# Input pieces, output-weight spreading and two-tile first matmuls in the opening of a planned attention-and-SoLU kernel

## The chip, the cores and the metric

The kernel runs on one core of a Trainium2 chip. The metric is device time in microseconds (us) of one launch; the median of 3 runs before the change is 1184.7 us. The engines are called PE (matmul; PEld is its weight load), DVE (vector), ACT (scalar), POOL (GpSimd) and SP (which issues the DMAs).

## The reference

There are four batches of 12608 tokens with 128 channels, 32 inducing points, and one feed-forward layer of width 1024 with a softmax gate (SoLU) and a layer norm.

```python
def mab(q, kv):                          # scale = 1 / sqrt(128)
    s = scale * (q @ kv.transpose(0, 2, 1))
    a = exp(s - s.max(-1)); a /= a.sum(-1) + 1e-09
    return a @ kv
x = mab(x, mab(I, x)).reshape(50432, 128)   # I: 32 inducing points per batch
h = x @ w_in                             # 128 -> 1024
e = exp(h - h.max(-1)); solu = h * e / (e.sum(-1) + 1e-09)
ln = (solu - mean(solu)) / sqrt(var(solu) + 1e-06) * g_ln
out = ln @ w_out                         # 1024 -> 128
```

w_in, w_out and g_ln come in the layout of the inputs; the two weight matrices are doubles of 1 MB each that the kernel rounds to float32 itself.

## The kernel before

**Work.** A batch is 99 tiles of 128 tokens. Part one (p1) loads a chunk of up to 16 tiles of x (12 in batch 0), turns them on PE, copies the turned tiles to SBUF (xT), makes the scores against the inducing points (L733), takes the maximum (L760, L766, L771, L792, L799), the exponent (ACT, L824), turns it back (L844), and gathers the weighted x (PE L850; DVE L882 adds it to acc). The turned x goes out to DRAM (xd) and comes back later as xT. When all chunks of a batch are through, combine (L910 to L936) divides by the sum (ACT accn, L915), makes h4 (DVE L919) and multiplies it by w_in (PE L933, copied to hs by ACT). Part two (p2) makes the second softmax of a chunk (PE L991, DVE L1001 and L1003, POOL L1006, ACT L1013) and turns the result into aT.

**The body.** For each tile: PE makes 1024 columns from aT and hs (L1233, "first matmuls"; K is 32 rows, so a tile takes two of the four row groups of the array), DVE multiplies and takes the minimum (hn, L1275), ACT takes the exponent (eu, L1286), POOL multiplies (L1290), ACT squares for the variance (L1301), DVE turns 32 x 32 blocks into vt (L1317). When a group of four tiles is turned, the products with w_out (L1473) follow in 32 steps for each of two pairs of row groups. A beat is one step on both pairs: eight matmul records, since each float32 matmul is recorded twice. Where only one pair has something to multiply, the step is a half beat. First matmuls, which use one pair, are issued with products on the other pair (`beats`, `whole`).

**Order.** No engine chooses at run time. The kernel yields operations with a cost, a priority (a low number goes first) and their predecessors to a Planner, which plays the four engines and SP through and writes the instructions down in that order; each engine then works through its list in order. What an instruction really waits for on the chip is only the data and buffers that it touches: the planner's tokens (BULK), events (loaded, turned) and priorities move instructions in the lists and make no wait of their own.

**The opening.** Until batch 0 is through part one, PSUM is eight small banks (bank_e). Batch 0's x is loaded with one DMA for 8 to 12 tiles. w_out is loaded, rounded on DVE, ACT and POOL (rounded), scaled by g_ln (ACT L492), its mean over the 1024 rows is taken on PE (L501) and subtracted on DVE (L506), and the 32-row quarters are spread over all partitions by PE (L544) and copied into wc by DVE and ACT (L522). All of that stands before handover, which closes the small banks and opens four two-bank tiles H for the body. Products need wc. Where the planner sees PE free for long it writes filler transposes (L557).

## Time and profile before

| | |
|---|---|
| median of 3 runs | 1184.7 us (1184.48 to 1186.08) |
| the profiled execution | 1182.92 us, of which the span of its instructions is 1181.1 us |
| PE, ACT, DVE, POOL busy | 97%, 93%, 91%, 90% of the span |
| first matmuls of the first tile | 52.87 us |
| first product with w_out | 76.74 us |
| mean granted PE clock | 0.994 |

A row of a timeline gives the start, the length, the engine, the line of the kernel, the operation and what it writes and reads; the brackets at its end say how long the engine idled before it and what ended that. Busy shares of all engines are high, so the question for each stretch is which wait ends last there.

### The profile page before, as it was taken

The numbers are of one execution on the slowest core, as the hardware profiler recorded it, in microseconds if no ns is written. First come the engines' busy times: TensorE is split into PE (matmuls) and PEld (weight loads), VectorE is DVE, ScalarE is ACT, GpSimd is POOL, SyncE is SP. The second block draws the span as 40 slices with busy tenths as digits, with TensorE's granted clock in tenths as the row PEclk, the third lists the DMA queues.
The fourth block names the chain that finished last, engine by engine and source line by source line (L and its number), as shares of the span: only waits on it lengthen the run. The fifth ranks groups of instructions, "written<-read, shape, count | busy, mean of one in ns | idle before, by whom it ended". The sixth has DMA issues, their size and how long they took to land.

```text
span 1181.1 us, 68196 instructions
## 1 busy us (share of the span) xinstructions
PE 1151.1 (97%) x30636; PEld 1055.0 (89%) x30636; DVE 1074.8 (91%) x1639; ACT 1102.6 (93%) x2191; POOL 1065.6 (90%) x612
## 2 busy tenths in 40 slices
PE   9999999999999999999999999999999999999996
PEld 7669989998889898999899999999988999999996
DVE  6799989898999899999899998999999999999981
ACT  5699899999999999999999999999999999999994
POOL 3399799898999989899899998989999999999994
PEclk9989999999999999999999999999999999999999
DMA  9532342522143433331423433341313131220103
GB/s 340 230 124 76 111 121 71 155 73 49 41 119 86 141 111 107 96 104 33 120 66 94 121 107 120 102 127 45 101 40 84 40 79 34 67 64 5 49 5 87
DMA packets 166884, 110.62 MB, mean 94 GB/s; under 512 B 78112, under 2 KB 131776, under 8 KB 166464
## 3 DMA queue, kind: packets, MB, share of 16 engines
q1 hardware_dynamic: 166592, 106.27, 31.0%
q8 instruction: 239, 3.92, 1.4%
q14 instruction: 53, 0.43, 0.1%
HBM read 53.51 MB, written 52.17 MB: 89 GB/s over the span
## 4 chain that ended last, share of the span: by engine, by line
PE 45%; POOL 23%; ACT 20%; issue 7%; DVE 3%; DMA 2%; SPq 0%; ACTq 0%; POOLq 0%; DVEq 0%
PE h L1473 32%; POOL eu L1290 16%; ACT sq L1301 9%; ACT eu L1286 6%; PE h L1233 4%; POOL spare L1290 3%; POOL spare L1547 3%; ACT spare L1286 1%; ACT xT L666 1%; ACT spare L1501 1%; PE h L850 1%; PE h L655 1%; ACT a L1013 1%; PE bank_e L557 1%; DMA dl<-dd 1%
## 5 line engine op out<-in xcount | busy, mean ns | idle before, releaser
L1473 PEld LDWEIGHTS h<-wc,vt 32*128 32x128 f32 (+1 forms) x25344 | 954.3, 185 | 45.8 <-issue 13.3
L1473 PE MATMUL h<-wc,vt 32*128 32x129 f32 (+1 forms) x25344 | 983.5, 273 | 10.4 <-ACT spare L1501 3.1
L1290 POOL TENSOR_TENSOR eu<-hn,eu 128x1024 f32<-128x1024 f32 x198 | 466.8, 2377 | 28.7 <-ACT eu L1286 27.7
L1233 PE MATMUL h<-hs,aT 32*128 32x512 f32 x1584 | 419.6, 607 | 6.0 <-DVE spare L1275 2.6
L1317 DVE STREAM_TRANSPOSE vt<-eu 128x1024 f32<-128x1024 f32 x327 | 397.7, 1229 | 11.4 <-POOL eu L1290 10.7
L1301 ACT ACTIVATE sq<-eu 128x1024 bf16<-128x1024 f32 x330 | 346.4, 1050 | 11.3 <-POOL eu L1290 6.5
L1290 POOL TENSOR_TENSOR eu<-spare,eu 128x1024 f32<-128x1024 f32 x132 | 311.7, 2379 | 11.2 <-ACT eu L1286 11.1
L1275 DVE TENSOR_SCALAR_CACHE_REDUCE hn<-h,rn 128x1024 f32<-128x1024 f32 x198 | 248.7, 1260 | 20.6 <-PE h L1233 12.2
L1275 DVE TENSOR_SCALAR_CACHE_REDUCE spare<-h,rn 128x1024 f32<-128x1024 f32 x198 | 248.2, 1260 | 20.7 <-PE h L1233 10.0
L1286 ACT ACTIVATE eu<-hn,nm 128x1024 f32<-128x1024 f32 x198 | 225.4, 1139 | 2.9 <-DVE hn L1275 2.7
L1290 POOL TENSOR_TENSOR spare<-spare 128x1024 f32<-128x1024 f32 x66 | 156.9, 2377 | 12.2 <-ACT spare L1286 12.2
L1286 ACT ACTIVATE eu<-spare,nm 128x1024 f32<-128x1024 f32 x132 | 150.4, 1140 | 2.3 <-DVE vt L1317 1.3
L1233 PEld LDWEIGHTS h<-hs,aT 32*128 32x128 f32 x1584 | 124.6, 186 | 27.5 <-DVE spare L1275 8.1
L1317 DVE STREAM_TRANSPOSE vt<-spare 128x1024 f32<-128x1024 f32 x65 | 80.0, 1231 | 2.0 <-POOL spare L1290 1.8
L1547 POOL TENSOR_TENSOR spare<-spare,fin 128x512 f32<-128x512 f32 x79 | 79.8, 1041 | 1.6
L1301 ACT ACTIVATE sq<-spare 128x1024 bf16<-128x1024 f32 x66 | 69.3, 1050 | 6.9 <-POOL spare L1290 5.3
L1286 ACT ACTIVATE spare<-spare,nm 128x1024 f32<-128x1024 f32 x66 | 75.2, 1140 | 0.4 <-DVE spare L1275 0.4
L1301 ACT ACTIVATION_READ_ACCUMULATOR sq<-eu 128x1 f32 x330 | 62.6, 190 | 0.0
L655 PE MATMUL h<-ident,xn 32*128 32x32 f32 x1188 | 53.6, 227 | 0.1
L655 PEld LDWEIGHTS h<-ident,xn 32*128 32x128 f32 x1188 | 51.1, 141 | 1.1 <-issue 0.8
L1501 ACT COPY spare<-h 128x774 f32<-128x774 f32 (+3 forms) x66 | 42.5, 646 | 9.3 <-PE h L1473 7.0
L666 ACT COPY xT<-h 128x1024 f32<-128x1024 f32 (+2 forms) x42 | 37.8, 900 | 1.1 <-PE h L655 1.1
(189 smaller groups left out, 849.6 us busy)
## 6 DMA issues: line engine op xcount, KB each, us to landing
out_dram<-spare SPq DMA_DIRECT2D x95, 256.0 KB, 3.3
xT<-xd SPq DMA_DIRECT2D x93, 256.0 KB, 3.8
xn<-in_x_dram SPq DMA_DIRECT2D x73, 256.0 KB, 3.7
xd<-xT SPq DMA_DIRECT2D x72, 256.0 KB, 2.6
dl<-dd SPq DMA_DIRECT2D x392, 1.0 KB, 2.3
xd<-vt SPq DMA_DIRECT2D x7, 768.0 KB, 10.2
spare<-in_x_dram SPq DMA_DIRECT2D x5, 768.0 KB, 9.3
dd<-qe SPq DMA_DIRECT2D x95, 4.0 KB, 2.1
```

What stands on the lines that cost most here:

```text
L557: nc.tensor.transpose(out=bank[:, :P], in_=ident, identity=ident)
L655: nc.tensor.transpose(out=tr[:, k * 512 + s * M : k * 512 + (s + 1) * M], in_=xn[r, s, :], identity=ident[r, r])
L666: lambda: nc.scalar.copy(xT.rearrange("c s (q t) -> c q s t", q=4)[:, 2 * w : 2 * w + 2, :n, :], tr.rearrange("c (k x) -> c k x", k=2)[:, ...
L1233: nc.tensor.matmul(hp[:, cols], lhsT=aT[rows, i // 2, :], rhs=hs[rows, cols], start=True, stop=True)
L1275: lambda: nc.vector.tensor_scalar(out=hn, in0=hp, scalar1=rn, scalar2=None, op0=ALU.mult, op1=ALU.min, accum_out=nm),
L1286: "ACT", 1133, lambda: nc.scalar.activation(e, hn, AF.Exp, bias=nm, scale=-1.0, accum_out=G["qe"][:, s, 1:2]), d, rel, srel,
L1290: d = yield Op("POOL", 2330, lambda: nc.gpsimd.tensor_tensor(out=e, in0=hn, in1=e, op=ALU.mult), de, prio=t + PR_MU)
L1301: "ACT", 1040, lambda: nc.scalar.activation(sq, e, AF.Square, scale=1.0 / 32.0, accum_out=G["qe"][:, s, 0:1]), d,
L1317: lambda: nc.vector.transpose(out=G["vtb"][:, : n * FF].rearrange("p (j s t) -> p j s t", j=M, s=n)[:, :, s, :], in_=e.rearrange("p (a f) ...
L1473: nc.tensor.matmul(op[:rows, a - 2 * w, :], lhsT=vt[q, k, :], rhs=wc[q, k, :], start=(k == 0), stop=(k == JB - 1))
L1501: return lambda: eng(to, at)
L1547: return lambda: eng.tensor_tensor(out=raw, in0=raw, in1=y[:, i0 : i0 + 4].unsqueeze(2).to_broadcast([rows, 4, C]), op=ALU.mult)
```

## The change

Seven things are changed together.

1. Batch 0's x is loaded in pieces of 4 tiles (256 KB), chunk after chunk, and a turn of 4 tiles needs only its own piece. The load of w_in stands after chunk 1 and that of w_out after chunk 4 (before: after chunk 3).
2. The mean of w_out, its subtraction and the spreading into wc move behind handover: they use tiles H of the body, two quarters to a tile, at priority WC_PR.
3. Until the first products are released (`flow["quiet"]`), the first matmuls of two tiles go out as one step on all four row groups (`mm1_two`, L1267 of the new kernel), and the turns of p1 and p2 are made on the whole array instead of by 32-row groups.
4. Products of a group are queued in the order of the groups (`began`), after wc is laid out.
5. The driver looks at the first unfinished group of each pair only.
6. In the planner: PE may pick an operation that is up to 100 ns late (SLACK), half beats weigh half in its picture of PE's clock (HALF), and four tiles instead of three are looked at for the next first matmuls (WINDOW_TILES).
7. Priorities: squares fall behind (PR_SQ from -4 to 6), fillers are written from 200 ns of idle time on, and w_out's steps and the weights' loads are moved. JS is an empty list, so the term with `wide` is always 0.

```diff
-FILL = 400
+FILL = 200
-LATE = -15
+LATE = -22
-PR_SQ = -4
+PR_SQ = 6
-SLACK = {"PE": 0, "ACT": 400, "DVE": 100, "POOL": 100, "SP": 0}
+SLACK = {"PE": 100, "ACT": 400, "DVE": 100, "POOL": 100, "SP": 0}
-WINDOW_TILES = 3
+WINDOW_TILES = 4
...
     def weights_out():
...
+        yield loaded[WOUT_AT]
         g = yield from rounded(wg2, w_out.bitcast(U32).rearrange("(k p) d -> p k d", p=P), conv2, None, conv2_free, WOUT_X)
...
-        yield turned[NP[0] - 1]
-        mp, rel = yield EARLY_PB.at(LATE)
+        if MEAN_H:
+            yield handed
+            where = H
...
+                hb, rel = yield H.at(WC_PR)
+                op = Op("PE", 950, None, d, rel, prio=WC_PR)
...
-        halves = [(0, GS), (GS, n)] if early and not k and n > GS else [(0, n)]
-        if not early:
-            halves = [(c, min(c + PIECE, n)) for c in range(0, n, PIECE)]
+        halves = [(c, min(c + PIECE, n)) for c in range(0, n, PIECE)]
+        if early and k:
+            yield loaded[k - 1]
...
-        if not early:
+        rows_only = not early and not flow["quiet"]
+        if rows_only:
             ways = [0, 1]
             for _ in range(2):
                 spawn(by_rows(ways), PRIO_P1(b, k))
-        for c0 in range(0, n if early else 0, most):
+        for c0 in range(0, 0 if rows_only else n, most):
...
-            mine = [p for q in stream for p in q if p["j"] < JB]
+            mine = [p for q in stream for p in [next((p for p in q if p["j"] < JB), None)] if p]
...
+                    if flow["quiet"] and len(left) > 1:
+                        two = [(s, part_of[b, ff_groups[j][0] + s]) for s in left[:2]]
...
+                        def mm1_two():
+                            hs = hT[b][1]
+
+                            for k in range(2):
+                                for (s, (ka, i)), hb in zip(two, (hp, hp2)):
+                                    r = i % 2 * 2
+                                    rows = slice((r + k) * M, (r + k + 1) * M)
+                                    cols = slice(k * 512, (k + 1) * 512)
+                                    aT = aT_of[(b, ka)]["aT"][0]
+                                    nc.tensor.matmul(hb[:, cols], lhsT=aT[rows, i // 2, :], rhs=hs[rows, cols], start=True, stop=True)
...
+        if turn_of[b, j]:
+            yield began[w][turn_of[b, j] - 1]
         yield PAIR[w].at(t)
+        yield wc_ready
+        flow["quiet"] = False
...
-        for e in (early_turned, wc_ready):
+        for e in (early_turned,) if MEAN_H else (early_turned, centred):
             d = yield e
             done += d
```

**PE, from w_in's product to the first matmuls of the body.** In the kernel before, the scores of the second p2 chunk (L991) are followed by the first matmuls of the tiles one by one (L1233, two rows of 512 columns for each tile, into one H tile each):

```order
L933 MATMUL bank_e_77<-w_in_sb,h_0_117 128x512
L557 MATMUL bank_e_72<-ident 128x128 x3
L1026 MATMUL bank_e_78<-ident,a_93 128x128 x2
L991 MATMUL h_730<-vt,h_0_117 32x256 x4
L1233 MATMUL h_732<-hs,aT_94 128x512 x2
L1233 MATMUL h_733<-hs,aT_94 128x512 x2
L1233 MATMUL h_730<-hs,aT_94 128x512 x2
L991 MATMUL h_731<-xT_86,h_0_117 32x512 x4
```

In the changed kernel the same place reads as follows (L959 is w_in's product, L1017 the scores, L1052 the turn of p2, L520 w_out's mean, L1267 the two-tile step):

```order
L959 MATMUL bank_e_78<-w_in_sb,h_0_117 128x512
L581 MATMUL bank_e_72<-ident 128x128 x3
L1052 MATMUL bank_e_79<-ident,a_93 128x128 x2
L1017 MATMUL h_709<-vt,h_0_117 32x256 x4
L520 MATMUL h_710<-hn_82,ones_mean 128x128 x8
L1267 MATMUL h_712<-hs,aT_94 128x512
L1267 MATMUL h_709<-hs,aT_94 128x512
L1052 MATMUL h_710<-ident,a_93 128x128 x4
```

The eight matmuls of the mean have moved from the opening to the place directly before the first matmuls, and two tiles share a step.

**DVE, from the second p2 chunk to the first group's transposes.** Before, hn of the first tiles (L1275) follows the maximum of the second p2 chunk at once:

```order
L1001 STREAM_TRANSPOSE s_1_90<-h_730 128x256
L1003 TENSOR_REDUCE mx_91<-s_1_90 128x8
L1275 TENSOR_SCALAR hn_81,nm_112<-h_732,rn_95 128x1024
L1275 TENSOR_SCALAR hn_80,nm_113<-h_733,rn_95 128x1024
L1095 TENSOR_REDUCE nr_92<-a_93 128x8
L1275 TENSOR_SCALAR hn_82,nm_114<-h_730,rn_95 128x1024
```

In the changed kernel (L1340 is hn, L525 the subtraction of w_out's mean, L1382 the transpose into vt, L543 a copy into wc):

```order
L1029 TENSOR_REDUCE mx_91<-s_1_90 128x8
L525 TENSOR_TENSOR hn_82<-h_710,hn_82 128x1024
L1124 TENSOR_REDUCE nr_92<-a_93 128x8
L1340 TENSOR_SCALAR hn_81,nm_112<-h_712,rn_95 128x1024
L1128 RECIPROCAL rn_97<-nr_92 128x8
L1340 TENSOR_SCALAR hn_80,nm_113<-h_709,rn_95 128x1024
L1027 STREAM_TRANSPOSE s_0_87<-h_711 128x512
L1029 TENSOR_REDUCE mx_88<-s_0_87 128x16
L1340 TENSOR_SCALAR spare,nm_114<-h_712,rn_95 128x1024
L1340 TENSOR_SCALAR spare,nm_115<-h_710,rn_95 128x1024
L1382 STREAM_TRANSPOSE vt<-eu 128x32x32
L543 COPY wc<-h_712 128x4x128
```

The subtraction now stands in front of the first hn, and copies into wc stand between the hn of the first tiles; the fourth transpose into vt comes after the tenth hn in both kernels.

**ACT, a stretch of the body after the first products.** Before (L1286 is the exponent, L1301 the square, L1072 a copy of turned aT):

```order
L1286 ACTIVATE eu,qe_106<-hn_80,nm_113 128x1024
L1072 COPY aT_96<-h_730 128x2x8x32
L1286 ACTIVATE eu,qe_106<-hn_82,nm_114 128x1024
L1301 ACTIVATE sq,qe_104<-spare 128x1024
L1286 ACTIVATE eu,qe_106<-spare,nm_115 128x1024
L1301 ACTIVATE sq,qe_106<-eu 128x1024 x3
```

In the changed kernel (L1351 is the exponent, L1366 the square, L691 a copy of turned x):

```order
L1351 ACTIVATE eu,qe_102<-spare,nm_112 128x1024
L1571 COPY spare<-h_711 128x2x3x129
L1351 ACTIVATE eu,qe_102<-hn_82,nm_114 128x1024
L1351 ACTIVATE spare,qe_102<-hn_81,nm_115 128x1024
L691 COPY xT<-h_709 128x2x16x32
L1366 ACTIVATE sq,qe_100<-eu 128x1024
L1366 ACTIVATE sq,qe_102<-eu 128x1024 x3
L1366 ACTIVATE sq,qe_102<-spare 128x1024
```

Squares have moved behind more exponents; over the whole list a square stands on average 3.1 exponents after its own instead of 2.6.

## Rows read from the trace of the kernel before

**Rows 1.** The page's first part: busy time of each engine, share of the span and instructions; and from its fourth part the shares of the engines in the chain that ended last.

```profile
PE 1151.1 (97%) x30636; PEld 1055.0 (89%) x30636; DVE 1074.8 (91%) x1639; ACT 1102.6 (93%) x2191; POOL 1065.6 (90%) x612
...
PE 45%; POOL 23%; ACT 20%; issue 7%; DVE 3%; DMA 2%; SPq 0%; ACTq 0%; POOLq 0%; DVEq 0%
```

**Rows 2.** Busy time of each engine by stretch: the stretch and its length, then PE, PEld, DVE, ACT, POOL with their instructions, the granted PE clock, the DMA share and GB/s.

```profile
20.00:30.00 10.00, 8.92 (x116) 6.49 (x114) 8.89 (x20) 7.05 (x17) 9.07 (x5) 1.00 1.05 400
30.00:40.00 10.00, 9.52 (x162) 7.73 (x163) 9.38 (x40) 6.08 (x19) 4.99 (x4) 1.00 1.01 419
40.00:50.00 10.00, 10.00 (x108) 7.42 (x107) 6.42 (x20) 5.51 (x18) 0.43 (x2) 1.00 0.46 176
...
60.00:70.00 10.00, 8.92 (x82) 3.81 (x79) 10.00 (x18) 9.78 (x20) 10.00 (x6) 0.93 0.37 127
```

**Rows 3.** DVE in order of time at the end of the opening.

```profile
41.02 0.22 DVE L792 TENSOR_SCALAR_CACHE_REDUCE small<-bank_e,m 128x4 f32<-128x4 f32 x1 [0.90 <-PE bank_e L771]
...
41.86 0.45 DVE L844 STREAM_TRANSPOSE spare<-spare 128x256 f32<-128x256 f32 x1 [0.42 <-ACT spare L824]
42.91 1.23 DVE L506 TENSOR_TENSOR hn<-bank_e,hn 128x1024 f32<-128x1024 f32 x1 [0.60 <-PE bank_e L501]
44.05 0.34 DVE L882 SCALAR_TENSOR_TENSOR acc<-acc,small,bank_e 128x128 f32<-128x128 f32 x1
...
45.67 1.29 DVE L522 COPY wc<-bank_e 128x512 f32<-128x512 f32 x2 [0.52 <-PE bank_e L544]
46.87 0.34 DVE L882 SCALAR_TENSOR_TENSOR acc<-acc,small,bank_e 128x128 f32<-128x128 f32 x1
```

**Rows 4.** The same stretch on ACT and PE, in order of time.

```profile
45.71 1.08 ACT L522 COPY wc<-bank_e 128x512 f32<-128x512 f32 x2 [2.75 <-PE bank_e L544]
47.51 0.40 ACT L915 ACTIVATE accn<-acc,small 128x128 f32<-128x128 f32 x1 [0.73 <-DVE small L913]
...
55.38 1.15 ACT L1286 ACTIVATE eu<-hn,nm 128x1024 f32<-128x1024 f32 x1
...
40.84 2.03 PE L501 MATMUL bank_e<-hn,ones_mean 128*128 128x128 f32 x16
...
52.30 0.64 PE L991 MATMUL h<-vt,h 128*32 128x256 f32 x8
52.87 1.99 PE L1233 MATMUL h<-hs,aT 32*128 32x512 f32 x12
```

**Rows 5.** DVE in order of time in the first part of the body.

```profile
54.05 1.28 DVE L1275 TENSOR_SCALAR_CACHE_REDUCE hn<-h,rn 128x1024 f32<-128x1024 f32 x1
...
55.26 1.28 DVE L1275 TENSOR_SCALAR_CACHE_REDUCE hn<-h,rn 128x1024 f32<-128x1024 f32 x1
...
56.79 1.27 DVE L1275 TENSOR_SCALAR_CACHE_REDUCE hn<-h,rn 128x1024 f32<-128x1024 f32 x1
...
66.04 0.66 DVE L1001 STREAM_TRANSPOSE s<-h 128x512 f32<-128x512 f32 x1
66.61 1.24 DVE L1275 TENSOR_SCALAR_CACHE_REDUCE hn<-h,rn 128x1024 f32<-128x1024 f32 x1
...
67.79 0.68 DVE L1003 TENSOR_REDUCE mx<-s 128x16 f32<-128x512 f32 x1
...
69.58 5.75 DVE L1317 STREAM_TRANSPOSE vt<-eu 128x1024 f32<-128x1024 f32 x5
75.31 1.28 DVE L1275 TENSOR_SCALAR_CACHE_REDUCE spare<-h,rn 128x1024 f32<-128x1024 f32 x1
```

**Rows 6.** PE in order of time around the first products, and a late stretch of products alone.

```profile
74.33 1.56 PE L733 MATMUL h<-xT,indT 128*32 128x512 f32 x8
76.74 2.50 PE L1473 MATMUL h<-wc,vt 32*128 32x129 f32 x48 [0.85 <-DVE spare L1275]
...
1159.97 6.66 PE L1473 MATMUL h<-wc,vt 32*96 32x129 f32 x228
```

**Rows 7.** As rows 2, in steps of 2 us before the first products.

```profile
66.00:68.00 2.00, 1.92 (x22) 0.98 (x23) 2.00 (x5) 2.00 (x5) 2.00 (x2) 1.00 0.00 0
68.00:70.00 2.00, 2.00 (x22) 1.20 (x23) 2.00 (x4) 1.91 (x4) 2.00 (x2) 0.64 0.00 0
...
72.00:74.00 2.00, 2.00 (x14) 0.83 (x12) 2.00 (x2) 2.00 (x3) 0.70 (x1) 0.50 0.00 0
74.00:76.00 2.00, 1.89 (x12) 0.20 (x8) 2.00 (x3) 2.00 (x4) 0.65 (x1) 0.65 0.39 132
76.00:78.00 2.00, 1.26 (x22) 1.29 (x24) 2.00 (x4) 2.00 (x5) 2.00 (x2) 1.00 0.42 119
```

**Rows 8.** Waits inside the body: who waited for whom, us in total, times, longest (ACT, from 80 to 1150 us); then PE's two large groups from 80 to 1150 us with busy us, mean ns and the idle time before them.

```profile
ACT sq L1301 <- POOL eu L1290: 4.7, 12, 1.0
ACT sq L1301 <- POOL spare L1290: 4.2, 4, 1.4
...
L1473 PE MATMUL h<-wc,vt 32*128 32x129 f32 (+1 forms) x24966 | 970.2, 273 | 9.3 <-ACT spare L1501 3.1 <-DVE spare L1501 2.1 <-DVE spare L1275 0.7
L1233 PE MATMUL h<-hs,aT 32*128 32x512 f32 x1532 | 407.3, 603 | 4.7 <-DVE spare L1275 2.0 <-ACT spare L1501 1.0 <-DVE hn L1275 0.9
```

**Rows 9.** SP's issues of loads, in order of time.

```profile
5.77 6.37 SPq L430 DMA_DIRECT2D hs<-in_moe_w_out_dram  x1
...
16.39 2.98 SPq L382 DMA_DIRECT2D xn<-in_x_dram  x4
```

More of the change, by code (lines that the diff above doesn't have):

```diff
@@ L41 @@
 SLOTS = 3
+STRETCH = 20
+JS = []
 PIECE = 4
 TOKENS = 4
+ETOK = 8
+WIN_AT = 1
+WOUT_AT = 4
+MEAN_H = 1
+PAIRED = 1
+HALF = 0.5
+WC_PR = -15
 TURN_ON = 90
@@ L202, in _step, with _pe @@
                 value = want.free.pop(0)
-    def _pe(self, start, cost):
+    def _pe(self, start, cost, weight=1.0):
         at = start
@@ L215, in _pe @@
             took = min(room, cost * rate)
-            self.busy[k] = self.busy.get(k, 0.0) + took
+            self.busy[k] = self.busy.get(k, 0.0) + took * weight
             at += took
@@ L253, in run @@
             op.fn()
-            end = start + (self._pe(start, op.cost) if eng == "PE" else op.cost)
+            end = start + (self._pe(start, op.cost, op.weight) if eng == "PE" else op.cost)
             clock[eng] = end
@@ L510, in weights_out @@
         )
-        give(EARLY_PB, mp, d)
+        give(where, mp, d)
+        plan.set(centred, d)
         freed = []
@@ L675, in by_rows @@
                 plan.set(copied, *ready)
-        if not early:
+        rows_only = not early and not flow["quiet"]
+        if rows_only:
             ways = [0, 1]
@@ L1026, in turn @@
                     nc.tensor.transpose(out=tr[:, q * P : (q + 1) * P], in_=both, identity=ident)
[L1028 removed]
+            dt = yield Op("PE", (0 if early else SWITCH) + 108.7 * pairs, turn, de, trel)
             d = yield Op(
@@ L1088, in p2 @@
         turned_too = Event()
-        if early:
-            assert n % 2 == 0 and pairs <= 4
+        whole_turn = early or flow["quiet"] and n % 2 == 0
+        if whole_turn:
+            assert n % 2 == 0 and pairs <= (4 if early else 8)
             spawn(turned_whole(), PRIO_P2(b, j))
-        for _ in range(0 if early else 2):
+        for _ in range(0 if whole_turn else 2):
             spawn(turned_rows(), PRIO_P2(b, j))
@@ L1131, in set_attention_then_solu_kernel @@
                 js = js[len(same) :]
+    turn_of = {bj: i for i, bj in enumerate((b, j) for b in range(NB) for j in order[b])}
+    began = [[Event() for _ in turn_of] for _ in range(2)]
     stream = [[], []]
-    flow = {"idle": Event(), "left": 2 * NB * NG - 2, "half": False, "took": 0}
+    flow = {"idle": Event(), "left": 2 * NB * NG - 2, "half": False, "took": 0, "quiet": bool(PAIRED)}
     def going(w, at):
@@ L1146, in beats @@
     def beats(count, pairs=(0, 1), also=None):
-        flow["took"] = 0
+        flow["took"], flow["weight"] = 0, 1.0
+        beat = 0
         for i in range(count):
@@ L1162, in beats @@
             full = went + bool(also) > 1
+            beat += 1 if full else HALF
+            flow["weight"] = beat / (i + 1)
             flow["took"] += BEAT + (TURN_ON if full and flow["half"] else 0)
@@ L1229, in whole @@
                         def whole(c):
-                            for k in range(2 if c == 0 else 0):
+                            for k in range(0 if c else 2):
                                 rows = slice((r + k) * M, (r + k + 1) * M)
@@ L1613, in handover @@
         late = pool("late", 1, PSUM, side="right")
-        for i in range(4):
-            give(H, buf([P, FF], f"h{i}", where=late), *done)
+        banks = [buf([P, FF], f"h{i}", where=late) for i in range(4)]
+        for hb in banks:
+            give(H, hb, *done)
         plan.scratch = (H,)
+        plan.set(handed, *done)
         for k in range(NP[0]):
```

98 lines of the change are left out of this document (65 added, 33 removed).

## The prediction

> **What bounds the kernel now.** I read the page's first part and the chain first: PE is busy for 97% of the span, but ACT, DVE and POOL for 90 to 93%, and the chain runs through PE, POOL and ACT for 45, 23 and 20% [rows 1]. No engine alone sets the end. Then the stretches: up to 40 us DVE is nearly full (8.89 and 9.38 of 10 us) while ACT and POOL have room; from 40 to 50 us even DVE falls to 6.42, a chain of single steps; from 60 us DVE, ACT and POOL are full together [rows 2]. So the opening is DVE's work and then a latency, and the body starts out limited by everything except PE. In the body PE idles before its two large groups for 9.3 + 4.7 us in 1070 us [rows 8], which makes the time at which products start, and what PE has to do from then on, the nearest thing to a bound.
>
> Last I read the end of the opening row by row [rows 3, 4]. Batch 0's last gathered x is added at 46.87 us, accn follows at 47.51 us, the first matmuls of the body at 52.87 us, the first hn at 54.05 us, and the first products at 76.74 us [rows 4 to 6]. Between the last scores and that last addition DVE does the subtraction of w_out's mean and two copies into wc, each after a wait for PE.
>
> **Step 1: accn comes earlier.** Out of the way go the subtraction (42.91 to 44.05, 1.14 us) and two copies (45.67 to 46.87, 1.20 us), 2.34 us of DVE, and the waits ahead of DVE's rows there, 0.90 + 0.42 + 0.60 + 0.52 = 2.44 us, may be filled or vanish [rows 3]. In the new order DVE has other chunks' additions and transposes to do while the last chunk's maximum and exponent are under way, and the last correction of w_out comes behind that maximum instead of ahead of it. So accn moves between 2.3 and 4.8 us; I take 4.6, since DVE has work in its list at each of the four waits.
>
> **The pieces of x** I cost at nothing. w_out's issue holds SP for 6.37 us and the last x is issued by 19.37 us [rows 9]; 13 further issues at some 0.45 us (four took 2.98 us with their waits) put that to some 25 us at most. What hides both the gain of early pieces and this delay is DVE, full until 40 us; without that cover the delay would cost up to 5.7 us.
>
> **Step 2: from accn to the first hn.** Before, this takes 54.05 - 47.51 = 6.54 us. Now the mean (40.84 to 42.87, about 1.9 us between its neighbours) stands on PE directly before the first matmuls, and the subtraction on DVE directly before the first hn. Behind L991 (end about 52.9 in the old clock) the mean ends at 54.8, the subtraction at 56.0, the sums nr (0.3: the third hn starts 1.53 us after the second instead of 1.21) at 56.4. The first hn is 2.3 us later against accn. Queued behind the subtraction on DVE are all hn, and for those ACT waits. Net: first hn 2.3 us earlier, about 51.8.
>
> **Step 3: from the first hn to the first products.** Before, 76.74 - 54.05 = 22.69 us: DVE made ten hn, then five transposes in a row (5.75 us), and the product still waited for the next hn (75.31 to 76.59) to give back its H tile [rows 5, 6]. In the new order DVE has ten hn (1.21 each, 12.1), four transposes (1.15, 4.6), three copies into wc (0.6 each, 1.8), two L1001 and two L1003 (0.57 and at most 0.68, 2.5) and small sums (0.9): 21.9 us, and the first product's tile is free by then. With 0.3 us to PE that is 22.2, so 0.5 us are won. **Products start 2.8 us earlier.** The two-tile steps and whole-array turns lie beside this: PE is ahead of DVE there (DVE and ACT full, [rows 2]), so I cost them at nothing. They cost something only where a slow clock lets PE fall behind, below.
>
> **Step 4: what PE has to do afterwards.** In the new order the scores of the next p1 chunk come after the first products instead of before: they took 1.56 us at a half-fast clock [rows 6, 7], about 1.1 us at full: +1.1. Counting beats in the order's list from the first product on (pairs of products on both sides, single ones, first matmuls, turns by rows) gives 4326 before and 4336 now. A beat takes 6.66 / 28.5 = 0.234 us (228 records, eight to a beat, [rows 6]), so 2.3 us more. Half beats stand where the other pair has nothing ready, so they may fill a wait: between 0 and 2.3. PE is in the chain for 45%: +1.0.
>
> PE's clock at that place: the granted clock was 0.64 at 68 to 70 us, 0.50 at 72 to 74 us and 1.00 again from 76 us, so the first product at 76.74 us met the full 2.4 GHz [rows 7]; by these rows nothing is added. The Trainium skill, "TensorE: Matmul & The Clock Gate", Part 1, says that the slow clock is the array's default and that it comes back when the work has gaps. The trace agrees that it comes back in this stretch; by that rule alone the changed opening, with shorter steps on PE and the same pauses, would hand the first products a slow array, and the sum would be that of the slower rival below, +3.9 instead of -2.6.
>
> **Step 5: squares later.** ACT waits 4.7 + 4.2 = 8.9 us in the body for POOL before a square [rows 8]. In the new list squares stand 3.1 exponents behind instead of 2.6, in longer runs. At best all 8.9 us go; at worst late squares hold the eu buffers and POOL waits as much for exponents. ACT and POOL share 43% of the chain; 0.43 x 8.9 = 3.8, and I take half, -1.9, since each square frees a buffer that an exponent needs. SLACK, the order of groups and the driver I cost at zero: bounds are the 14.0 us of PE idle above, below, and as much above, by new waits of 0.1 us each.
>
> **The sum.** -2.8 + 1.1 + 1.0 - 1.9 = -2.6 us against the profiled execution's own 1182.92 us (span 1181.1 us and 1.8 us around it): 1180.3. The median is 1.8 us above that execution, so I forecast 1184.7 - 2.6 = 1182.1, say 1182.0 us. About 0.2%, 2.4 us, is what a measurement of this kernel can tell from no change, and the forecast sits just beyond it.
>
> **Rivals.**
>
> *The head's gain is used up before the body (no change).* ACT is the fuller engine: the first exponent comes 2.3 us earlier (before: 55.38), but five of eight copies into wc now lie behind it on ACT (0.54 each by the pair of 1.08 us, [rows 4]), 2.7 us. Then ACT stands at the same point of its work as before, and the end at 1184 to 1186 us. The same comes out if accn moves by 2.3 us only. For it speaks ACT at 9.78 of 10 us from 60 us on [rows 2]; against it that squares can wait, since nothing in the first group's products needs them.
>
> *PE pays at the start of products (slower).* The clock fell to the lower level (1.2 GHz) at 68 to 70 us, after a stretch in which PE ran mostly half-array first matmuls, and was at the full 2.4 GHz again by 76 us, 0.7 us before the first product [rows 7]. Two-tile steps and short turns give PE less time at work per tile; if the low stretch, 6 to 7 us long, now lies behind the first products, half of it, 3.3 us, is lost where PE is waited for. With all 2.3 us of extra beats and the scores, and without the relief of step 5: -2.8 + 3.3 + 2.3 + 1.1 = +3.9, 1188.6 us. It decides from a loss of 1.8 us on, since -2.8 + 2.3 + 1.1 = +0.6 and +2.4 is where slower begins. For it speaks that the low stretch ended only 0.7 us early; against it that the mean, the spreading and the turns of the next chunk are additional whole-array or half-array work in the same stretch.
>
> *The body runs better (faster by more).* If all of the 8.9 us of ACT's waits goes and the beats cost nothing: -2.8 + 1.1 - 8.9 = -10.6, 1174.1 us. For it: POOL stands in the chain for 23% and is fed by exponents. Against it: planned beats are no fewer.
>
> **Chances.** Forecast, products start earlier and the body keeps its pace: 0.40 (1179 to 1184; 0.31 of it beyond 0.2%, 0.09 within). Gain used up: 0.25 (0.20 within, 0.03 faster, 0.02 slower). PE pays: 0.22, all slower but 0.01. Better body: 0.13, faster. Faster 0.47, same 0.30, slower 0.23. A new list reshuffles 1070 us of the body, so the range takes in the better body and the slow start with a margin of the 1 to 2 us that runs differ: 1174 to 1190 us, the likeliest case's own range being 1179 to 1184.
>
> **What would show it.** Step 1: accn at 42.5 to 43.5 us, and no subtraction ahead of the last addition on DVE. Step 2: the first hn at 51 to 52.5 us, 8.9 us behind accn, with the subtraction directly before it. Step 3: the first product at 73.5 to 74.5 us. Step 4: records of products alone at the same mean, PE idle in the body near 14 us. Step 5: ACT's waits for POOL before squares under 5 us. The prediction is wrong if the last x lands after 29 us, if the clock's low stretch reaches past the first product, or if ACT, not PE, is last to be ready there; and the largest risk is that the new body list is simply better or worse by more than the opening's whole 2.8 us.

## The result, and the profile after

The changed kernel takes **1195.0 us** (median of 4 runs, 1194.4 to 1195.5) against 1185.0 us for the kernel before on the same chip; the ratio is 1.0087, with an interval of 1.0062 to 1.0113. It is 10 us slower; 1182.0 us, with a range of 1174 to 1190 us, was forecast. One launch of `b_cost_p4`, below, took 5189 us and is left out of every figure here. The profiled execution took 1195.54 us (span 1193.8 us).

The page of the changed kernel, its first part and its chain by engine, to be read beside [rows 1]:

```profile
PE 1155.9 (97%) x30543; PEld 1057.8 (89%) x30543; DVE 1077.7 (90%) x1638; ACT 1112.7 (93%) x2190; POOL 1061.0 (89%) x612
...
ACT 31%; PE 27%; POOL 22%; issue 8%; DVE 5%; DMA 5%; SPq 1%; ACTq 0%; POOLq 0%; DVEq 0%
```

ACT has gone from 20 to 31% of the chain and PE from 45 to 27%, while ACT's busy time has grown by 10.1 us although it has one instruction fewer. That is the first hint. Next the end of the opening, in order of time on ACT, DVE and PE of the changed kernel (L506 is w_out's gain, L466 a late correction of w_out's rounding, L941 accn):

```profile
43.81 0.40 ACT L506 ACTIVATE hn<-hn,g_sb 128x128 f32<-128x128 f32 x1 [2.12 <-DVE hn L466]
44.20 0.40 ACT L941 ACTIVATE accn<-acc,small 128x128 f32<-128x128 f32 x1
...
42.59 1.18 DVE L466 SCALAR_TENSOR_TENSOR hn<-aT,hn 128x1024 f32<-128x1024 int32 x1
43.69 0.15 DVE L938 TENSOR_SCALAR small<-bank_e 128x1 f32<-128x1 f32 x1
43.76 0.34 DVE L908 SCALAR_TENSOR_TENSOR acc<-acc,small,bank_e 128x128 f32<-128x128 f32 x1
...
51.23 1.23 DVE L525 TENSOR_TENSOR hn<-h,hn 128x1024 f32<-128x1024 f32 x1 [1.05 <-PE h L520]
52.70 1.27 DVE L1340 TENSOR_SCALAR_CACHE_REDUCE hn<-h,rn 128x1024 f32<-128x1024 f32 x1
...
68.36 0.69 DVE L543 COPY wc<-h 128x512 f32<-128x512 f32 x1 [0.83 <-ACT wc L543]
73.18 2.37 DVE L1382 STREAM_TRANSPOSE vt<-eu 128x1024 f32<-128x1024 f32 x2
...
75.69 2.50 PE L1542 MATMUL h<-wc,vt 32*128 32x129 f32 x60 [1.24 <-DVE vt L1382]
```

accn comes at 44.20 us (before 47.51), the first hn at 52.70 (54.05), the first product at 75.69 (76.74). So the opening is 1.05 us shorter, and from the first product to the end of the span the changed kernel takes 1193.8 - 75.69 = 1118.1 us instead of 1181.1 - 76.74 = 1104.4. **The body lost 13.7 us.**

The clock of the stretch before the products, to be read beside [rows 2, 7] (columns as there), does not explain it:

```profile
60.00:70.00 10.00, 6.46 (x40) 2.73 (x40) 9.06 (x15) 9.25 (x19) 10.00 (x6) 1.00 0.21 78
...
68.00:70.00 2.00, 1.61 (x12) 0.31 (x6) 1.64 (x2) 2.00 (x5) 2.00 (x2) 1.00 0.00 0
```

It stayed at the upper level (2.4 GHz) although PE worked less there than before. Nor do waits on PE explain all of it (80 to 1150 us, beside [rows 8]; L1542 is the product, L1297 the first matmul): 9.5 + 7.6 = 17.1 us instead of 14.0. But POOL waits much longer for exponents, 52.4 + 10.4 = 62.8 us; in the kernel before it was 34.1 + 12.2 = 46.3 in the same stretch.

```profile
L1542 PE MATMUL h<-wc,vt 32*128 32x129 f32 (+1 forms) x24530 | 972.2, 273 | 9.5 <-ACT spare L1571 4.4 <-DVE spare L1571 1.3 <-issue 1.3
L1297 PE MATMUL h<-hs,aT 32*128 32x512 f32 x1520 | 404.4, 604 | 7.6 <-ACT spare L1571 2.3 <-DVE spare L1340 2.2 <-DVE hn L1340 1.2
```

The waits inside the body (us in total, times, longest), first the kernel before, then the changed kernel:

```profile
POOL eu L1290 <- ACT eu L1286: 34.1, 36, 2.5
...
POOL spare L1290 <- ACT spare L1286: 12.2, 9, 4.3
```

```profile
POOL eu L1355 <- ACT eu L1351: 52.4, 39, 3.8
POOL spare L1355 <- ACT spare L1351: 10.4, 8, 3.0
...
ACT sq L1366 <- POOL eu L1355: 8.8, 11, 1.2
```

### The profile page after: what moved, and what is told of

It is laid out like the page before. It is cut to its first block, busy times and chain, and to the rows that moved or that the text cites. A ratio compares the mean times of both kernels' runs of the same rounds, so it can differ in the third digit from the quotient of the medians.

```text
span 1193.8 us, 68083 instructions
## 1 busy us (share of the span) xinstructions
PE 1155.9 (97%) x30543; PEld 1057.8 (89%) x30543; DVE 1077.7 (90%) x1638; ACT 1112.7 (93%) x2190; POOL 1061.0 (89%) x612
## 4 chain that ended last, share of the span: by engine, by line
ACT 31%; PE 27%; POOL 22%; issue 8%; DVE 5%; DMA 5%; SPq 1%; ACTq 0%; POOLq 0%; DVEq 0%
PE h L1542 20%; POOL eu L1355 16%; ACT sq L1366 14%; ACT eu L1351 10%; POOL spare L1355 3%; PE h L1297 2%; POOL spare L1617 2%; ACT spare L1351 2%; DMA dl<-dd 1%; DVE vt L1382 1%; ACT spare L1571 1%; DMA dd<-qe 1%; DVE spare L1340 1%; ACT xT L691 1%; DMA spare<-in_x_dram 1%
## 5 line engine op out<-in xcount | busy, mean ns | idle before, releaser
L1542 PE MATMUL h<-wc,vt 32*128 32x129 f32 (+1 forms) x25344 | 998.4, 273 | 10.8 <-ACT spare L1571 4.4
L1542 PEld LDWEIGHTS h<-wc,vt 32*128 32x128 f32 (+1 forms) x25344 | 963.8, 184 | 45.3 <-issue 20.8
L1355 POOL TENSOR_TENSOR eu<-spare,eu 128x1024 f32<-128x1024 f32 x198 | 466.0, 2375 | 26.8 <-ACT eu L1351 25.6
L1297 PE MATMUL h<-hs,aT 32*128 32x512 f32 x1528 | 406.5, 604 | 7.6 <-ACT spare L1571 2.3
L1382 DVE STREAM_TRANSPOSE vt<-eu 128x1024 f32<-128x1024 f32 x327 | 399.2, 1231 | 15.4 <-POOL eu L1355 14.7
L1366 ACT ACTIVATE sq<-eu 128x1024 bf16<-128x1024 f32 x330 | 346.8, 1051 | 19.8 <-POOL eu L1355 10.7
L1355 POOL TENSOR_TENSOR eu<-hn,eu 128x1024 f32<-128x1024 f32 x132 | 313.6, 2376 | 31.2 <-ACT eu L1351 31.2
L1340 DVE TENSOR_SCALAR_CACHE_REDUCE spare<-h,rn 128x1024 f32<-128x1024 f32 x198 | 248.4, 1262 | 23.9 <-PE h L1297 10.2
L1340 DVE TENSOR_SCALAR_CACHE_REDUCE hn<-h,rn 128x1024 f32<-128x1024 f32 x198 | 248.3, 1260 | 22.0 <-PE h L1297 9.4
L1351 ACT ACTIVATE eu<-spare,nm 128x1024 f32<-128x1024 f32 x198 | 225.7, 1141 | 3.2 <-DVE spare L1340 2.6
L1355 POOL TENSOR_TENSOR spare<-hn,spare 128x1024 f32<-128x1024 f32 x66 | 156.8, 2376 | 10.4 <-ACT spare L1351 10.4
L1351 ACT ACTIVATE eu<-hn,nm 128x1024 f32<-128x1024 f32 x132 | 150.6, 1141 | 0.9 <-DVE hn L1340 0.2
L1297 PEld LDWEIGHTS h<-hs,aT 32*128 32x128 f32 x1528 | 120.6, 185 | 27.2 <-DVE spare L1340 7.1
L1382 DVE STREAM_TRANSPOSE vt<-spare 128x1024 f32<-128x1024 f32 x65 | 80.0, 1231 | 2.6 <-POOL spare L1355 2.6
L1351 ACT ACTIVATE spare<-hn,nm 128x1024 f32<-128x1024 f32 x66 | 75.3, 1141 | 0.2
L1366 ACT ACTIVATE sq<-spare 128x1024 bf16<-128x1024 f32 x66 | 69.4, 1051 | 3.4 <-POOL spare L1355 1.6
L1366 ACT ACTIVATION_READ_ACCUMULATOR sq<-eu 128x1 f32 x330 | 62.2, 188 | 0.0
L691 ACT COPY xT<-h 128x1024 f32<-128x1024 f32 (+2 forms) x40 | 35.8, 895 | 3.1 <-PE h L679 2.6
```

The lines of the kernel that those rows point to most:

```text
L691: lambda: nc.scalar.copy(xT.rearrange("c s (q t) -> c q s t", q=4)[:, 2 * w : 2 * w + 2, :n, :], tr.rearrange("c (k x) -> c k x", k=2)[:, ...
L1297: nc.tensor.matmul(hp[:, cols], lhsT=aT[rows, i // 2, :], rhs=hs[rows, cols], start=True, stop=True)
L1340: lambda: nc.vector.tensor_scalar(out=hn, in0=hp, scalar1=rn, scalar2=None, op0=ALU.mult, op1=ALU.min, accum_out=nm),
L1351: "ACT", 1133, lambda: nc.scalar.activation(e, hn, AF.Exp, bias=nm, scale=-1.0, accum_out=G["qe"][:, s, 1:2]), d, rel, srel,
L1355: d = yield Op("POOL", 2330, lambda: nc.gpsimd.tensor_tensor(out=e, in0=hn, in1=e, op=ALU.mult), de, prio=t + PR_MU)
L1366: "ACT", 1040, lambda: nc.scalar.activation(sq, e, AF.Square, scale=1.0 / 32.0, accum_out=G["qe"][:, s, 0:1]), d,
```

## The experiments

In the expectations, theory A is that squares put off by PR_SQ 6 hold the exponents' buffers; B that another setting of the planner does the harm; C that the body's list was dealt out anew and the old one was a good draw; D that the opening hands the body a worse start; E came later, from the trace.

### One setting or one part at a time

`b_sq6`: the kernel before with `PR_SQ = 6`. 

> The kernel before with one number changed: PR_SQ from -4 to 6, so that squares fall behind exponents. Theory A (late squares hold buffers of the exponents, ACT waits for POOL and POOL for ACT): the body gets most of the changed kernel's loss, 1192 to 1197 us, POOL's idle time before its multiplication grows from 52 to 65 us or more, and ACT's before squares from 11 to 20 us. Rival B (the loss is in other settings): 1183 to 1187 us. Rival C (any new list of the body moves the time by several us, whatever was set): off 1185 by more than 2.5 us in either direction, with no common sign over the runs.

`a_sq4`: the changed kernel with `PR_SQ = -4`. 

> The changed kernel with PR_SQ back at -4, everything else as changed. Theory A: the body's loss goes, products start at 75.7 us as in the changed kernel, and the end is at 1183 to 1187 us. Rival B: 1193 to 1197 us. Rival C: anywhere between 1183 and 1200 us, and not the mirror image of the run that sets PR_SQ alone in the kernel before.

`a_open`: the opening's edits alone.

```diff
-HALF = 0.5
+HALF = 1.0
-PR_SQ = 6
+PR_SQ = -4
-SLACK = {"PE": 100, "ACT": 400, "DVE": 100, "POOL": 100, "SP": 0}
+SLACK = {"PE": 0, "ACT": 400, "DVE": 100, "POOL": 100, "SP": 0}
-WINDOW_TILES = 4
+WINDOW_TILES = 3
-            mine = [p for q in stream for p in [next((p for p in q if p["j"] < JB), None)] if p]
+            mine = [p for q in stream for p in q if p["j"] < JB]
-        if turn_of[b, j]:
-            yield began[w][turn_of[b, j] - 1]
```

> The changed kernel with all of the body's settings as before (PR_SQ -4, PE's SLACK 0, WINDOW_TILES 3, HALF 1.0, the driver looking at every group, no order of groups by began); the pieces of x, the spreading behind handover, the two-tile steps and the whole-array turns stay. Theory A or B (the loss is in the settings of the body): products start near 75.7 us and the end is at 1182 to 1185 us. Rival D (the opening hands the body a worse start, since 3.5 us are lost by the first 5% of the products): 1192 to 1197 us. Rival C: off 1184 by more than 2.5 us.

`a_mix1`: the changed kernel with `JS = [(0, 0)] * 6 + [(2, 1)] * 60`. 

> The changed kernel with JS filled from its seventh stretch on (width 2, turn 1): from 120 us on every priority is moved by a fixed mixed amount of at most one tile's rank, and nothing else is touched. It measures how far a reshuffle of the list alone moves the time. Rival C: at least 4 us away from the changed kernel's 1195.0 us, in either direction. Theories A, B and D: within 3 us of 1195.0 us, since settings and opening are the same.

Measured: `b_sq6` 1205.6 us (ratio to before 1.0176, 1.0143 to 1.0210), `a_sq4` 1192.5 (1.0071, 1.0046 to 1.0096), `a_open` 1194.8 (1.0086, 1.0058 to 1.0114), `a_mix1` 1201.7 (1.0148, 1.0115 to 1.0180). PR_SQ alone costs the kernel before twice what the whole change costs, more than theory A's 1192 to 1197 us; yet taking it back gives the changed kernel only 2.5 us, and the two intervals overlap. `a_mix1`, which reshuffles the list and leaves settings and opening alone, moves the time by 6.7 us, as C has it. `a_open` is still slow, but it decides less than it seems to. Its first product comes at 81.17 us (its row stands under step 4 below) and not near 75.7, as A and B had assumed, and from there to the end of its span of 1193.1 us it takes 1111.9 us, 6.2 less than the changed kernel and 7.5 more than the kernel before. So B is not refuted by it, and its 1194.8 us lie in the range of D as well as of C. Nothing that touches the list came near the kernel before, which speaks for C; C was tried next by itself. What answers B and D for the changed kernel is `a_two_sq`, further below.

### The same settings, another draw

One planned cost is moved by 4 ns, the time with which the planner books POOL's multiplication (the two pages show 2375 to 2379 ns for it):

```diff
-        d = yield Op("POOL", 2330, lambda: nc.gpsimd.tensor_tensor(out=e, in0=hn, in1=e, op=ALU.mult), de, prio=t + PR_MU)
+        d = yield Op("POOL", 2326, lambda: nc.gpsimd.tensor_tensor(out=e, in0=hn, in1=e, op=ALU.mult), de, prio=t + PR_MU)
```

`b_cost_m4` and `b_cost_p4` are the kernel before with 2326 and 2334, `a_cost_m4` and `a_cost_p4` the changed kernel.

> The kernel before with one planned cost changed by 4 ns: POOL's multiplication is booked with 2326 instead of 2330 ns (both traces show 2376), nothing else. No setting changes, but the planner deals the body out anew. Counted in the list from the first product on, it has 4357 beats (before 4326, changed 4336), 31 more, at 0.234 us each 7.3 us. Theory C (before's list is one lucky draw among its equals; what the change lost is that draw, and not a setting): 1188 to 1200 us beside a before of 1183. Theory A or D (the loss comes from PR_SQ or from the opening, a redraw is harmless): within 2.5 us of before.

> The same with 2334 instead of 2330 ns: 4357 beats. Theory C: 1188 to 1200 us beside a before of 1183, not the same time as with 2326. Theory A or D: within 2.5 us of before.

> The changed kernel with POOL's multiplication booked with 2326 instead of 2330 ns: 4319 beats, 17 fewer than the changed kernel. Theory C: off the changed kernel's 1195 us by more than 2.5 us, and by the beats on the fast side, 1187 to 1193 us. Theory A or D: within 2.5 us of 1195.

> The changed kernel with 2334 instead of 2330 ns: 4340 beats. Theory C: 1190 to 1200 us; the mean of the changed kernel's redraws below the mean of those of the kernel before by some 4 us, since they have some 25 beats fewer. Theory A or D: within 2.5 us of 1195 us, and above both redraws of the kernel before.

Measured: `b_cost_m4` 1194.9 us (1.0089, 1.0059 to 1.0120), `b_cost_p4` 1197.0 (1.0109, 1.0078 to 1.0139), `a_cost_m4` 1209.3 (1.0206, 1.0166 to 1.0245), `a_cost_p4` 1199.8 (1.0127, 1.0092 to 1.0162). So the kernel before is a good draw of its own settings: 4 ns in a planned cost lose as much as the change did. The beats were no guide: `a_cost_m4` has 17 fewer than the changed kernel and is 14 us slower. And C may not be all: both redraws of the changed kernel are slower than both of the kernel before, where by the beats their mean was expected to be lower. That of `a_cost_p4` and `b_cost_p4`, though, is within their intervals.

### Squares in a row

What sets the lists with PR_SQ 6 apart stands on ACT. The changed kernel, ACT in order of time (L1366 is the square with its read of the accumulator, L691 a copy, L1351 the exponent):

```profile
200.15 0.99 ACT L691 COPY xT<-h 128x1024 f32<-128x1024 f32 x1
201.04 1.06 ACT L1366 ACTIVATE sq<-eu 128x1024 bf16<-128x1024 f32 x1
202.00 0.19 ACT L1366 ACTIVATION_READ_ACCUMULATOR sq<-eu 128x1 f32 x1
202.28 1.06 ACT L1366 ACTIVATE sq<-spare 128x1024 bf16<-128x1024 f32 x1
203.24 0.19 ACT L1366 ACTIVATION_READ_ACCUMULATOR sq<-spare 128x1 f32 x1
203.52 1.06 ACT L1366 ACTIVATE sq<-eu 128x1024 bf16<-128x1024 f32 x1
204.49 0.19 ACT L1366 ACTIVATION_READ_ACCUMULATOR sq<-eu 128x1 f32 x1
...
207.54 1.06 ACT L1366 ACTIVATE sq<-eu 128x1024 bf16<-128x1024 f32 x1
208.50 0.19 ACT L1366 ACTIVATION_READ_ACCUMULATOR sq<-eu 128x1 f32 x1
208.59 1.13 ACT L1351 ACTIVATE eu<-hn,nm 128x1024 f32<-128x1024 f32 x1
```

In these rows an exponent follows a square after 208.59 - 207.54 = 1.05 us and starts inside the accumulator's read; a square follows a square after 202.28 - 201.04 = 1.24 us, 0.09 us behind the end of that read (202.00 + 0.19). Over the whole trace none of the 141 squares directly behind a square starts less than 1.10 us after it, and the median is 1.24. The rows carry no bracket. A reason stands in the code: all squares write the same scratch buffer `sq`, whose content nobody reads (the variance goes out by the accumulator). In ACT's list with its waits, a square behind an exponent waits for POOL alone, the squares behind it for ACT's own semaphore too:

```
L1351 ACTIVATE eu,qe_104<-spare,nm_114 128x1024 [waits DVE_49,Activation_49]
L1366 ACTIVATE sq,qe_102<-eu 128x1024 [waits Pool_49]
L1366 ACTIVATE sq,qe_102<-eu 128x1024 [waits Activation_49,Pool_49]
L1366 ACTIVATE sq,qe_104<-spare 128x1024 [waits Activation_49,Pool_49]
```

The Trainium skill, "ScalarE: Activation LUTs", section "What ACT_TABLE_LOAD costs", gives 186 ns + 0.833 ns for each element for such an instruction and says that ones back to back overlap by some 93 ns. An estimate from it is 1.04 us for a square, and the rows show 1.06. The read at 202.00 starts 0.10 us before the square ahead of it ends, and the exponent at 208.59 as long before the read ahead of it ends, which agrees; a square behind a read, at 202.28, does not overlap it at all.

So theory E is that the second of two squares in a row waits until the first has written the scratch buffer. The kernel before has the same pairs, only fewer: 70 of 396 squares stand directly behind a square in its list, 141 in the changed kernel. Two rows of the kernel before, 1.23 us apart:

```profile
315.18 1.05 ACT L1301 ACTIVATE sq<-eu 128x1024 bf16<-128x1024 f32 x1
316.41 1.06 ACT L1301 ACTIVATE sq<-spare 128x1024 bf16<-128x1024 f32 x1
```

`a_two_sq` and `b_two_sq` give both kernels two scratch buffers in turn. The order on every engine stays as it is.

```diff
-    sq = buf([P, FF], "sq", BF16)
+    sqs = bufs(2, [P, FF], "sq", BF16)
+    turns = iter(range(10**6))
...
-                "ACT", 1040, lambda: nc.scalar.activation(sq, e, AF.Square, scale=1.0 / 32.0, accum_out=G["qe"][:, s, 0:1]), d,
+                "ACT", 1040, lambda: nc.scalar.activation(sqs[next(turns) % 2], e, AF.Square, scale=1.0 / 32.0, accum_out=G["qe"][:, s, 0:1]), d,
```

> The changed kernel with two scratch buffers for the squares, taken in turn, instead of one; the order on every engine is unchanged. In the trace of the changed kernel a square that follows a square starts 1.24 us after it, one that is followed by an exponent lets it start after 1.04 to 1.06; there are 141 such pairs against 70 in the kernel before. Theory E (the second square waits until the first has written the one scratch buffer; squares in a row therefore cost 0.2 us each, and PR_SQ 6 makes rows of squares): pairs at 1.04 us, ACT 25 to 28 us of time freed, of which about ACT's share of the chain (31%) reaches the end: 1184 to 1190 us. Rival C (draw alone) or a pitch that belongs to squares and not to the buffer: 1193 to 1197 us.

> The kernel before with two scratch buffers for the squares, order unchanged. Theory E: 70 pairs x 0.2 us = 14 us of ACT freed, of which ACT's share of the chain (20%) reaches the end: 1179 to 1183 us beside a before of 1184, faster than before by 1 to 5 us. Rival: the same as before within 1.5 us.

Measured: `a_two_sq` **1180.1 us** (1.0087 becomes 0.9944, 0.9928 to 0.9961), `b_two_sq` 1181.4 (0.9959, 0.9940 to 0.9978). Both beat the kernel before, which took 1186.0 us beside them. The changed kernel gains 15 us from an edit that moves no instruction; that is more than theory E gave it (1184 to 1190 us), since more than ACT's share of the chain reached the end. It keeps every setting, the opening and the order of the changed kernel, its first product comes at 75.56 us, and it beats the kernel before: so neither another setting (B) nor the opening's start (D) is needed for the changed kernel's loss. Of its 141 pairs 121 now start less than 1.10 us apart. The same place in `a_two_sq`, with 1.05 and 1.04 us between squares (L1367 is the square); then the page, where POOL's idle time before its multiplication, the last but one column, has gone from 26.8 + 31.2 us (first two rows, changed kernel) to 19.5 + 28.0 and PE is back in the chain:

```profile
200.33 1.05 ACT L1367 ACTIVATE sq<-eu 128x1024 bf16<-128x1024 f32 x1
201.29 0.19 ACT L1367 ACTIVATION_READ_ACCUMULATOR sq<-eu 128x1 f32 x1
201.38 1.04 ACT L1367 ACTIVATE sq<-spare 128x1024 bf16<-128x1024 f32 x1
202.33 0.19 ACT L1367 ACTIVATION_READ_ACCUMULATOR sq<-spare 128x1 f32 x1
202.42 1.04 ACT L1367 ACTIVATE sq<-eu 128x1024 bf16<-128x1024 f32 x1
```

```profile
L1355 POOL TENSOR_TENSOR eu<-spare,eu 128x1024 f32<-128x1024 f32 x198 | 466.0, 2375 | 26.8 <-ACT eu L1351 25.6
L1355 POOL TENSOR_TENSOR eu<-hn,eu 128x1024 f32<-128x1024 f32 x132 | 313.6, 2376 | 31.2 <-ACT eu L1351 31.2
```

```profile
PE 1149.7 (98%) x30543; PEld 1056.5 (90%) x30543; DVE 1076.0 (91%) x1638; ACT 1101.4 (93%) x2190; POOL 1061.2 (90%) x612
...
PE 48%; POOL 16%; ACT 15%; DVE 9%; issue 8%; DMA 3%; SPq 1%; ACTq 0%; POOLq 0%; DVEq 0%
...
L1356 POOL TENSOR_TENSOR eu<-spare,eu 128x1024 f32<-128x1024 f32 x198 | 466.2, 2376 | 19.5 <-ACT eu L1352 19.0
L1356 POOL TENSOR_TENSOR eu<-hn,eu 128x1024 f32<-128x1024 f32 x132 | 313.7, 2376 | 28.0 <-ACT eu L1352 27.1
```

ACT's busy time falls by 11.3 us. That is less than the 141 x 0.2 = 28 us of the pairs, because some half of a pair's 0.2 us was the gap behind the accumulator's read, which counts as idle.

### More draws with either PR_SQ

`a_sq4_cost_m4` is the changed kernel with PR_SQ -4 and the cost 2326, `b_sq6_cost_p4` the kernel before with PR_SQ 6 and 2334.

> The changed kernel with PR_SQ back at -4 and POOL's multiplication booked with 2326 instead of 2330 ns, one more draw of the new opening with squares as before. If PR_SQ costs several us on the average of draws (theory A with E as its mechanism): near the other runs with -4 (1192 to 1198 us), below those with 6 (1195 to 1209 us). If there is only the draw (C): anywhere from 1190 to 1210 us.

> The kernel before with PR_SQ at 6 and POOL's multiplication booked with 2334 instead of 2330 ns. Theories A and E: 1199 to 1210 us, square-after-square pairs well above 70. C alone: anywhere from 1190 to 1210 us.

Measured: 1192.9 us (1.0049, 1.0029 to 1.0068) and 1204.1 us (1.0147, 1.0119 to 1.0176). With these, and both openings together, the mean ratio of the five new lists with PR_SQ -4 is 1.0081 (82 pairs on the average) and that of the six with 6, the changed kernel among them, 1.0149 (139 pairs): 0.7%, 8 us, for PR_SQ on the average of draws. The two sets overlap (1.0049 to 1.0109 and 1.0087 to 1.0206), and by the gains for each pair below, 0.06 to 0.12 us, the 57 further pairs make up an estimated 3 to 7 of the 8 us.

### Two buffers under other draws

The same two-buffer edit in four lists that had run with one.

> The changed kernel with two scratch buffers and PR_SQ back at -4 (83 squares directly behind squares in the list instead of 141). With one buffer this list took 1192.5 us, 2.5 less than with 6. Theory E alone: 83 pairs x 0.2 us = 16.6 us of ACT are freed instead of 28, so it gains less than the changed kernel did (15 us), and ends at 1182 to 1186 us, no faster than the changed kernel with two buffers (1180.1): the number 6 is harmful only through the buffer. Theory A without E (late squares hold the exponents' buffers as well): faster than 1180 by 2 us or more.

> The kernel before with PR_SQ 6 and two scratch buffers (93 pairs in the list). With one buffer 1205.6 us. Theory E alone explains 93 x 0.2 = 18.6 us of ACT of which about half reached the end in the changed kernel: 1194 to 1197 us. If all of PR_SQ's harm were the buffer: 1180 to 1185 us. The rest, if any, is the draw of the list or the eu buffers: in that run an exponent starts 1.17 us after a square instead of 1.04.

> The slowest draw of the changed kernel (POOL's multiplication booked with 2326 ns, 1209.3 us, 148 pairs) with two scratch buffers. Theory E: it gains as much as the changed kernel did, 13 to 17 us, and ends at 1192 to 1196 us; the 12 to 16 us that then remain against the changed kernel with two buffers are the draw. If draws differ by the buffer alone: 1178 to 1183 us.

> The draw of the kernel before with 2326 ns (1194.9 us, 91 pairs) with two scratch buffers. Theory E: 18 us of ACT freed, 4 to 9 us at the end: 1186 to 1191 us; what remains against the kernel before with two buffers (1181.4) is the draw. If draws differ by the buffer alone: 1180 to 1183 us.

Ratios to the kernel before, with one buffer and with two, and the pairs in the list:

| list | pairs | one buffer | two buffers (interval) | gain |
|---|---|---|---|---|
| before | 70 | 1 | 0.9959 (0.9940 to 0.9978) | 0.41% |
| before, PR_SQ 6 | 93 | 1.0176 | 1.0101 (1.0073 to 1.0128) | 0.75% |
| before, 2326 ns | 91 | 1.0089 | 1.0042 (1.0021 to 1.0063) | 0.47% |
| changed | 141 | 1.0087 | 0.9944 (0.9928 to 0.9961) | 1.43% |
| changed, PR_SQ -4 | 83 | 1.0071 | 1.0023 (1.0007 to 1.0039) | 0.48% |
| changed, 2326 ns | 148 | 1.0206 | 1.0107 (1.0082 to 1.0131) | 0.99% |

The four new medians are 1186.9, 1196.9, 1196.8 and 1189.4 us, in the order of the expectations; the first and the third miss theory E's ranges by 1 us on the slow side. The direction of theory E holds in all six: every list gains, and the two with by far the most pairs gain most, 0.06 to 0.12 us for each pair of the 0.2 us that it held ACT. Only for the draw of the kernel before with 2326 ns do the intervals with one buffer and with two still touch.

With two buffers PR_SQ 6 is faster than -4 in the changed kernel (0.9944 against 1.0023) and slower in the kernel before (1.0101 against 0.9959), and draws differ by as much. The traces show what a second scratch buffer leaves in place. Where squares stand late, an exponent is often given the very eu buffer that the square directly ahead of it has just read; it waits for ACT's own semaphore then, and starts 1.16 to 1.19 us after the square instead of 1.04. That is a buffer held by a late square, as in theory A, but it is ACT itself that waits. `b_two_sq_sq6` (L1287 is the exponent, L1302 the square):

```profile
713.24 1.04 ACT L1302 ACTIVATE sq<-eu 128x1024 bf16<-128x1024 f32 x1
714.19 0.19 ACT L1302 ACTIVATION_READ_ACCUMULATOR sq<-eu 128x1 f32 x1
714.41 1.15 ACT L1287 ACTIVATE eu<-spare,nm 128x1024 f32<-128x1024 f32 x1
```

There are 155 such starts in it, 155 in `b_sq6`, 37 in the changed kernel and 1 in the kernel before. At 0.13 us each that is an estimate of 20 us of ACT for the two with PR_SQ 6 in the kernel before, which would fit the 17 us between them with two buffers; no run takes this wait out, so that it is the cause is argued and not shown.

What the two waits do not explain is the rest of the draw, 0.9944 to 1.0107 with two buffers. One piece of it is the end of the list. In `a_two_sq` the last plain products are done before the last tile's own matmuls (L1461); in `a_two_sq_cost_m4` 16 products are left behind them, and two evacuations and the whole of the last group's finish follow. `a_two_sq`, PE in order of time, then `a_two_sq_cost_m4`:

```profile
1140.41 9.65 PE L1543 MATMUL h<-wc,vt 32*128 32x129 f32 x310
...
1167.35 3.84 PE L1461 MATMUL h<-xn,vt 128*128 128x129 f32 x32 [0.59 <-ACT vt L1446]
```

```profile
1151.61 9.44 PE L1543 MATMUL h<-wc,vt 32*128 32x129 f32 x306
...
1178.84 3.84 PE L1461 MATMUL h<-xn,vt 128*128 128x129 f32 x32 [0.59 <-ACT vt L1446]
1182.61 0.70 PE L1543 MATMUL h<-wc,vt 32*96 32x129 f32 x16
```

From the first of these rows to the end of the span it is 1178.8 - 1140.4 = 38.4 us in one and 1196.8 - 1151.6 = 45.2 in the other, 6.8 of the 18.0 us between the two spans. The first products of the two are 0.35 us apart (75.56 and 75.91 us), so some 11 us stand in the body; which of its waits the draw decides stays open.

## Why the prediction was wrong

**The step that failed is step 5.** It put the later squares down as -1.9 us, with everything between a gain of 8.9 us and an equal loss by held buffers. The waits that it meant to remove did not go: ACT's waits for POOL before squares were to fall under 5 us, and came to 8.8 + 0.4 = 9.2 instead of 8.9. Its worst case was too small as well: POOL's waits for exponents grew by 62.8 - 46.3 = 16.5 us. The larger mistake is that the step priced the waits and not the instructions. It said that the new list has its squares "in longer runs", and costed a run at nothing; the trace of the kernel before showed squares in a row 1.23 us apart instead of 1.05, without a wait in brackets, and 71 more of these are 14 us of ACT, which at 93% has few gaps to put them in. With one buffer the changed kernel stands at +0.87%, with two buffers in both kernels at 0.9944 / 0.9959 = -0.15%, which these runs cannot tell from no change. So between these two lists the one scratch buffer accounts for the loss in the medians; at equal clocks some 2.4 us remain (last section).

**Step 1** was right in kind and too large: accn is 3.3 us earlier, within 2.3 to 4.8, but 4.6 was taken because DVE's waits were to be filled. One was filled by the wrong thing, the 1.18 us of L466 directly before the last addition, and a piece of w_out's gain (0.40 us) stands directly before accn on ACT. The pieces of x cost nothing that can be seen, as said: PE and its weight load waited for them for 2.2 + 0.8 us in all, and PE's last turn of batch 0's x ends at 33.52 us, before at 33.79.

**Step 2** held: 8.50 us from accn to the first hn where 8.9 was worked out, with the mean on PE (49.14 to 51.12 us) and the subtraction ahead of it.

**Step 3** gave 22.99 us from the first hn to the first product instead of 22.2. DVE was not full there (9.06 of 10 us); one of its copies into wc waited 0.83 us for ACT's. The order of events was as read from the list: the product waited for the fourth transpose, not for a tile. Products start 1.05 us earlier instead of 2.8.

**Step 4**: the slow clock did not reach the first products in the changed kernel; the granted clock was 1.00 from 60 us on. So the rival in which PE pays at the start of the products did not come true here, and the slower time has another cause. In `a_open` the place that this rival named did come out: the granted clock is 0.50 from 80 to 90 us, and the first product stands in that stretch, at 81.17 us. That it comes so late is not the clock's doing, which was 0.99 from 70 to 80 us. The Trainium skill, "TensorE: Matmul & The Clock Gate", Part 1, says that the slow clock comes back when the work has gaps. The changed kernel's trace does not bear out the use that the prediction made of it: PE was busy for 6.46 of 10 us and the clock stayed up, while in the kernel before it fell to 0.64 where PE was busy for 2.00 of 2 us [rows 7]. The windows of `a_open`, then its PE in order of time:

```profile
70.00:80.00 10.00, 7.57 (x46) 2.58 (x43) 10.00 (x21) 9.91 (x17) 8.37 (x5) 0.99 0.62 209
80.00:90.00 10.00, 10.00 (x122) 9.23 (x126) 9.96 (x14) 9.82 (x20) 7.45 (x4) 0.50 0.30 74
```

```profile
81.17 3.13 PE L1540 MATMUL h<-wc,vt 32*128 32x129 f32 x24
```

The extra beats (+1.0 taken) can't be told apart from waits in the result. The edit of the driver, costed at zero in step 5, is zero by itself: made alone in the kernel before, it leaves every row of its list as it is, and so does that of WINDOW_TILES, which the prediction does not name. SLACK alone deals the list out anew.

**The range** was too narrow by the prediction's own words. It named a redrawn list of the body as the largest risk, bounded what SLACK, the order of groups and the driver do to the list by 14 us to either side, and then let the range reach 8 us. Two redraws of the kernel before with nothing but one planned cost moved lost 10.6 and 12.8 us by their medians. The chances of a redraw were not symmetric: none of the eleven other lists with one buffer, the changed kernel's among them, beat the kernel before. That would be so if its list was chosen among many for its time, which no run here shows.
